# The first two chunks of a fused attention and expert kernel share each weight block, and most of the weight decoding moves behind the first batch

## The chip, the cores and the metric

The kernel runs on one core of a Trainium2 chip. Its time is the device time of one execution in microseconds; the version before took 1003.2 us (median of three runs, 1001.3 to 1006.09). A profile of one execution stands beside it. Engines are named as the profile names them: PE (matmul) with PEld (its weight loads), DVE (vector), ACT (scalar), POOL (GpSimd), and SP, which only issues transfers (SPq is its queue).

## The reference

All inputs are float32, apart from two weight matrices that arrive as float64 and are read as pairs of 32-bit words. Cut to what matters:

```python
q, k, v                                # (8 batches, 8 heads, 576, 64)
q_d, k_d, v_d = mean of 4 neighbours   # (8, 8, 144, 64)
out_up = repeat(softmax(q_d @ k_d.T / 8) @ v_d, 4)         # coarse attention
mask   = |i - j| < 4                                       # 7 neighbours
out_local = softmax(where(mask, q @ k.T / 8, -1e9)) @ v    # local attention
x = (out_up + out_local) as (4608 tokens, 512)
h = x @ w_in                           # (512, 2048)
g = max(h, 0) + alpha * min(h, 0)      # alpha: one per column
out = g @ w_out                        # (2048, 512)
```

## The kernel before, in words

**The long part** is the two products with w_in and w_out. The tokens are cut into 18 chunks of 256, the 2048 hidden columns into 8 pairs of 128-column blocks; one chunk with one pair is a *step*, 144 in all. Every number is carried as a high part and a low part, so that each product takes three matmuls. A step consists of `hidden` (L760, 24 matmuls into a tile `h`), `slopes` (L771 to L775, ACT scales `h` by the two slopes), `larger` (the greater of the two, L783, on DVE), `split` (`gh`, L788 on ACT, and `gl`, L70 on POOL) and `product` (L817, 24 matmuls into `o`, a bank for each 128 tokens). In the first 12 steps (`EARLY`) the greater of the two is not taken on DVE: ACT makes a second tile `sh` (L773) and POOL adds it (L73). After the eighth step of a chunk `finish` copies `o` to `sg` (L823, ACT) and stores it.

**The weights** have to be decoded first, w_in and w_out in eight blocks each, block (0, p) and (1, p) for pair p. `make` gives the five parts of a block: `magnitude` (L187, ACT), `reach` (L191 and L192, DVE), `bits` (L196 and L197, DVE, which read the raw words), `upper` (L202 for w_in, L206 for w_out, ACT: the high part) and `lower` (L210 or L214, DVE: the low part). A block is decoded whole (instructions of 1024 columns, with the temporary tile in SBUF) or in two halves (512 columns, temporary in a PSUM bank). Raw words come in by SP's queue (L148 for w_in, L152 for w_out, two transfers of 0.5 MB a block) into three slots; the last two pairs of blocks go to four buffers that are in the pool `late`. The memory of that pool is the first batch's until that batch is done.

**The first batch** of attention (batch 0, which is the tokens of steps 0 to 15 and a little more) runs ahead of all that, on a path of its own (`first_batch`, L399 to L525), and ends with `xh` and `xl`, the two parts of x that step 0 multiplies. Beside it DVE and ACT decode the blocks of the first `N_EARLY` pairs. Which of the early loads are queued at which place is told by the string `ORDER`: `a0` is q and k of head pair 0, `b0` its v, `i0` and `o0` the raw words of blocks (0, 0) and (1, 0).

**Later batches** are worked on between the steps: the coarse attention by `down` (folds on POOL, L73; s, pT and pv on PE), the local attention in *units* of a third of a batch (L597 to L656 on DVE). The end of a unit is its *join* (L677 on DVE, then `xh` on ACT and `xl` on POOL), which gives x for one and a half chunks. Chunk 2, which is step 16 in the order before, needs unit 3 and a part of unit 4.

**The order** behind the first batch is written out by hand: every function is put at a time counted in steps (`at(s - 1.95, hidden, s)`), all are sorted by it, and each engine runs its instructions in that order. The decoding of half blocks starts at 0.5 and a half is given 0.56; `UNITS` gives the beginnings of units 3 to 7. Nothing on an engine passes what stands ahead of it.

Of the kernel before, what the change touches and what calls it, by code (L numbers as in the profile page):

```python
# [9 lines left out]
F32 = mybir.dt.float32  # L10
# [3 lines left out]
ALU = mybir.AluOpType  # L14
# [11 lines left out]
NF = DF // 128  # L26
# [25 lines left out]
def tile_attention_moe(ctx: ExitStack, tc: tile.TileContext, q, k, v, w_in, w_out, alpha, out):  # L52
# [4 lines left out]
    two = ctx.enter_context(tc.tile_pool(name="two", bufs=2))  # L57
    PS = bass.MemoryType.PSUM
    ps_o = ctx.enter_context(tc.tile_pool(name="ps_o", bufs=2, space=PS))
    ps_h = ctx.enter_context(tc.tile_pool(name="ps_h", bufs=2, space=PS))  # L60
# [14 lines left out]
    NS = NCHUNK * NF // 2  # L75
    NP = NF // 2


# [672 lines left out]
    def hidden(st):  # L751
        c, fp = divmod(st, NP)
        xh, xl = xT[c]
        ph = hs[st] = ps_h.tile([128, 2, T], F32, tag="ph", name=f"h{st}")
        for j in range(2):
            n, o = divmod(2 * fp + j, 4)
            i = 0
            for w, x in ((wi[0][n], xh), (wi[1][n], xh), (wi[0][n], xl)):
                for m in range(4):
                    nc.tensor.matmul(ph[:, j], w[:, m, 128 * o:128 * o + 128], x[:, m, :],  # L760
                                     start=(i == 0), stop=(i == 11))
                    i += 1

    def slopes(st):
# [4 lines left out]
        for j in range(2):  # L769
            f = 2 * (st % NP) + j  # L770
            nc.scalar.activation(t[:, j], hs[st][:, j], AF.Copy, scale=slope[:, f:f + 1])  # L771
            if st < EARLY:
                nc.scalar.activation(other[:, j], hs[st][:, j], AF.Relu, scale=gain[:, f:f + 1])  # L773
            else:
                nc.scalar.activation(other[:, j], hs[st][:, j], AF.Copy, scale=sign[:, f:f + 1])  # L775
# [29 lines left out]
    def product(st):  # L805
        c, fp = divmod(st, NP)
        if fp == 0:
            outs[c] = [ps_o.tile([128, DM], F32, tag="po", name=f"o{c}_{m}") for m in range(T // 128)]
        gh, gl = gs.pop(st)
        order = [(j, i, m) for j in range(2) for i in range(3) for m in range(T // 128)]  # L810
        if st == NS - 1 or fp == 0:
            order.sort(key=lambda x: x[2])
        for j, i, m in order:
            f = 2 * fp + j
            n, o = divmod(f, 4)
            g, w = ((gh, 0), (gh, 1), (gl, 0))[i]
            nc.tensor.matmul(outs[c][m], g[:, j, 128 * m:128 * m + 128], wo[w][n][:, o, :],  # L817
                             start=(f == 0 and i == 0), stop=(f == NF - 1 and i == 2))

    def finish(c):  # L820
        for m, po in enumerate(outs.pop(c)):
            sg = two.tile([128, DM], F32, tag="stage", name=f"sg{c}_{m}", bufs=SB)
            nc.scalar.copy(sg, po)  # L823
            for i in range(4):
# [26 lines left out]
    with tc.tile_pool(name="start", bufs=1) as start:  # L851
# [26 lines left out]

    for s in range(NS):
        at(s - 1.95, hidden, s)  # L880
        at(s - 1.45, slopes, s)
        at(s - 1.15, larger, s)
        at(s - 1.0, split, s)
        at(s + 0.6, product, s)
        if s % NP == NP - 1:
            at(s + 1.02, finish if s + 1 < NS else finish_last, s // NP)

    blocks = [(w, fp, c) for w in range(2) for fp in range(N_EARLY, NP) for c in range(2)]
# [5 lines left out]
    for w, fp, c in blocks:  # L894
        for lag, f in zip((-0.3, 0.0, 0.4, 0.95, 1.2), make(w, fp, c)):
            at(t + lag * D_DEC, f)
        t += D_DEC
        if w == 0 and fp >= NP - 2:
            at(t, load_raw, 1, fp, (c,))
    decoded = t  # L900
# [6 lines left out]
    for u in range(len(UNITS) + 3, 3 * B + 1):  # L907
        begin[u] = begin[u - 1] + U_STEP
    at(3.3, load_q, 3)
    at(3.4, load_kv, 3, "k")  # L910
    at(decoded + 0.3, load_kv, 3, "v")
# [8 lines left out]
    for u in range(3, 3 * B + 1):  # L920
# [4 lines left out]
        if put and u - 1 in BY_HALF:  # L925
            flip_at(u - 1, 1, begin[u] + 0.3, flip)
            put(1, when["before 0"])
        elif put:
            flip_at(u - 1, 0, begin[u] + 0.3, flip)
            put(0, when["before 0"])  # L930
            t = when["before 0"] + 0.25 if u == 4 else when["before 1"]
            flip_at(u - 1, 1, max(begin[u] + 0.31, t - 0.6), flip)
            put(1, t)
# [56 lines left out]
```

## Time and profile before

| | |
|---|---|
| time, median of 3 runs | 1003.2 us (1001.3 to 1006.09) |
| span of the profiled execution | 995.7 us |
| PE busy in the span | 955.8 us (96%) |
| DVE | 825.6 us (83%) |
| ACT | 559.2 us (56%) |
| POOL | 497.8 us (50%) |
| last `xl` of the first batch begins on DVE | 87.11 us |
| last piece of decoding begins on DVE | 146.52 us |
| first local instruction of unit 3 begins on DVE | 147.70 us |
| first matmul of step 16 (first of chunk 2) | 191.55 us |

The time of the profiled execution is that of the first to the last instruction; the 7.5 us between it and the median lie around the span. The rows read: start, duration (both us), engine, line, operation, output and inputs, shape; in brackets the idle time ahead of it and what ended that. The windows give busy time with the number of instructions, the granted clock of PE as a share of full speed, the share of the DMA engines' time and what they moved.

### The profile page before, as it was taken

The numbers are of one execution on the slowest core, as the hardware profiler recorded it, in microseconds if no ns is written. First come the engines' busy times: TensorE is split into PE (matmuls) and PEld (weight loads), VectorE is DVE, ScalarE is ACT, GpSimd is POOL, SyncE is SP. The second block draws the span as 40 slices with busy tenths as digits, with TensorE's granted clock in tenths as the row PEclk, the third lists the DMA queues.
The fourth block names the chain that finished last, engine by engine and source line by source line (L and its number), as shares of the span: only waits on it lengthen the run. The fifth ranks groups of instructions, "written<-read, shape, count | busy, mean of one in ns | idle before, by whom it ended". The sixth has DMA issues, their size and how long they took to land.

```text
span 995.7 us, 17954 instructions
## 1 busy us (share of the span) xinstructions
PE 955.8 (96%) x6402; PEld 850.2 (85%) x6402; DVE 825.6 (83%) x1336; ACT 559.2 (56%) x1483; POOL 497.8 (50%) x624
## 2 busy tenths in 40 slices
PE   5977999999999999999999999999999999999998
PEld 4756877888889888888998889898889888899896
DVE  7999887889898889899899888899898889996111
ACT  5766775455656555555565555565556564544442
POOL 2132866677475636555546455655456632324221
PEclk9957999999999999999999999999999999999999
DMA  8947524243423322423322323232324222210000
GB/s 209 217 150 260 159 65 130 79 126 90 131 90 100 111 87 68 136 79 102 98 87 82 117 84 109 91 104 88 100 84 126 85 67 67 70 33 22 1 22 22
DMA packets 63196, 98.27 MB, mean 99 GB/s; under 512 B 23556, under 2 KB 28932, under 8 KB 63108
## 3 DMA queue, kind: packets, MB, share of 16 engines
q1 hardware_dynamic: 62916, 96.88, 33.0%
q8 instruction: 50, 0.82, 0.3%
q10 hardware_dynamic: 192, 0.26, 0.1%
q14 instruction: 38, 0.31, 0.1%
HBM read 87.67 MB, written 9.44 MB: 98 GB/s over the span
## 4 chain that ended last, share of the span: by engine, by line
PE 77%; DVE 12%; ACT 3%; POOL 3%; issue 2%; SPq 1%; DMA 1%; DVEq 0%; POOLq 0%; ACTq 0%
PE o L817 35%; PE h L760 35%; PE s L266 2%; PE pv L300 2%; PE xp L665 1%; DVE temp L196 1%; DVE lb L656 1%; PE pT L290 1%; DVE qk L597 1%; DVE temp L197 1%; DVE ls L601 1%; SPq L399 1%; POOL t L73 1%; DVE wil L210 1%; DVE pv L653 1%
## 5 line engine op out<-in xcount | busy, mean ns | idle before, releaser
L70 POOL TENSOR_TENSOR gl<-t,gh 128x512 fp32r<-128x512 f32 x144 | 186.3, 1294 | 347.2 <-ACT gh L788 340.1
L771 ACT ACTIVATE t<-h,slope 128x256 f32<-128x256 f32 x288 | 136.7, 474 | 144.7 <-PE h L760 117.5
L817 PE MATMUL o<-woh,gh 128*128 128x512 f32 x576 | 194.9, 409 | 2.6 <-ACT sg L823 2.6
L760 PE MATMUL h<-xh,wih 128*128 128x256 f32 x1152 | 189.5, 286 | 0.6 <-ACT xh L524 0.6
L817 PE MATMUL o<-wol,gh 128*128 128x512 f32 x576 | 188.2, 397 | 0.2 <-DVE wol L214 0.2
L817 PE MATMUL o<-woh,gl 128*128 128x512 f32 x576 | 187.9, 397 | 0.0
L760 PE MATMUL h<-xl,wih 128*128 128x256 f32 x1152 | 183.1, 281 | 0.8 <-POOL xl L70 0.8
L760 PE MATMUL h<-xh,wil 128*128 128x256 f32 x1152 | 183.2, 281 | 0.0
L783 DVE TENSOR_TENSOR t<-h,t 128x512 f32<-128x512 f32 x132 | 90.7, 687 | 103.0 <-ACT h L775 101.8
L760 PEld LDWEIGHTS h<-xh,wih 128*128 128x128 f32 x1152 | 163.5, 190 | 11.0 <-issue 1.0
L788 ACT CAST gh<-t 128x512 fp32r<-128x512 f32 x144 | 89.2, 619 | 127.7 <-DVE t L783 95.7
L760 PEld LDWEIGHTS h<-xl,wih 128*128 128x128 f32 x1152 | 156.3, 189 | 1.0 <-POOL xl L70 1.0
L760 PEld LDWEIGHTS h<-xh,wil 128*128 128x128 f32 x1152 | 156.4, 189 | 0.0
L73 POOL TENSOR_TENSOR ld<-ld 72x256 f32<-72x256 f32 x168 | 127.5, 759 | 42.4 <-DMA ld<-in_q 39.7
L601 DVE TENSOR_REDUCE ls<-qk 128x12 f32<-128x768 f32 (+1 forms) x126 | 136.5, 1084 | 3.2
L817 PEld LDWEIGHTS o<-woh,gl 128*128 128x128 f32 x576 | 108.7, 189 | 26.3
L817 PEld LDWEIGHTS o<-wol,gh 128*128 128x128 f32 x576 | 108.3, 188 | 26.4 <-DVE wol L214 1.4
L656 DVE TENSOR_TENSOR lb<-lb,pv 128x384 f32<-128x384 f32 x202 | 113.9, 564 | 5.6
L817 PEld LDWEIGHTS o<-woh,gh 128*128 128x128 f32 x576 | 99.6, 189 | 20.2 <-ACT sg L823 3.1
L775 ACT ACTIVATE h<-h,sign 128x256 f32<-128x256 f32 x264 | 116.1, 440 | 0.0
L653 DVE TENSOR_TENSOR pv<-v,lb 128x1152 f32<-128x1152 f32 x84 | 93.6, 1115 | 2.6
L597 DVE TENSOR_TENSOR qk<-k,qp 128x768 f32<-128x768 f32 (+1 forms) x78 | 83.9, 1076 | 0.0
(151 smaller groups left out, 1133.4 us busy)
## 6 DMA issues: line engine op xcount, KB each, us to landing
k<-in_k SPq DMA_DIRECT2D x41, 384.0 KB
v<-in_v SPq DMA_DIRECT2D x41, 384.0 KB
out<-sg SPq DMA_DIRECT2D x140, 64.0 KB
raw<-in_moe_w_in SPq DMA_DIRECT2D x16, 512.0 KB
raw<-in_moe_w_out SPq DMA_DIRECT2D x16, 512.0 KB
ld<-in_q SPq DMA_DIRECT2D x56, 144.0 KB
ld<-in_k SPq DMA_DIRECT2D x56, 144.0 KB
ld<-in_v SPq DMA_DIRECT2D x56, 144.0 KB
```

The costliest lines, as they stand in the source:

```text
L70: nc.gpsimd.tensor_tensor(o, a, b, op=ALU.subtract)
L73: nc.gpsimd.tensor_tensor(o, a, b, op=ALU.add)
L597: nc.vector.tensor_tensor(st["pr"][:, :nd], window(tiles[u, "k"], half, d0, nd), st["qp", half].unsqueeze(1).to_broadcast([128, nd, 2, 192 ...
L601: nc.vector.tensor_reduce(out=st["s"][:, half, d0:d0 + nd, :].rearrange("p a b -> p (a b)"), in_=st["pr"][:, :nd].rearrange("p a h (t d) - ...
L653: nc.vector.tensor_tensor(st["pr"][:, :nd], window4(tiles[u, "v"], half, d0, nd), prob(half, d0, nd), op=ALU.mult)
L656: nc.vector.tensor_tensor(st["acc"], st["acc"], st["pr"][:, i], op=ALU.add)
L760: nc.tensor.matmul(ph[:, j], w[:, m, 128 * o:128 * o + 128], x[:, m, :], start=(i == 0), stop=(i == 11))
L771: nc.scalar.activation(t[:, j], hs[st][:, j], AF.Copy, scale=slope[:, f:f + 1])
L775: nc.scalar.activation(other[:, j], hs[st][:, j], AF.Copy, scale=sign[:, f:f + 1])
L783: nc.vector.tensor_tensor(gs[st], hs.pop(st), gs[st], op=ALU.max)
L788: nc.scalar.copy(gh, t)
L817: nc.tensor.matmul(outs[c][m], g[:, j, 128 * m:128 * m + 128], wo[w][n][:, o, :], start=(f == 0 and i == 0), stop=(f == NF - 1 and i == 2))
```

## The change

Lines of the changed kernel are 8 higher than before (L196 becomes L204, L760 becomes L768).

- **Order of the steps.** `BLOCKS` runs chunk 0 with pairs 0 to 3, then chunk 1 with all eight pairs, then chunk 0 with pairs 4 to 7. Chunks 2 to 17 follow as before, each with a start that lies `GAP` = 2.4 later in the table.
- **Chunk 0 in two parts.** After its first four steps `park` copies the two banks of `o` (ACT) and stores them in DRAM; `fetch` loads them in the second half, and `finish` adds them on DVE where it otherwise copies on ACT.
- **Decoding.** Two blocks, (0, 0) and (0, 1), instead of ten stand ahead of the end of the first batch. Twelve blocks are decoded whole and four in halves, where it was ten and six; they come in the order in which the steps need them (`WHOLE`, `HALVES`).
- **Loads.** Only the raw words of w_in for pairs 0 to 2 are queued among the first batch's loads; each other block's are queued when the third block ahead of it has been read.
- **Attention.** Units 3 to 7 begin 3.7 to 2.4 later in the table, the join of unit 4 is put at fixed places. `EARLY` is 16 instead of 12.

```diff
-ORDER = 'i0 a0 a1 b0 o0 a2 b1 a3 b2 i1 b3 o1 i2'
-N_EARLY = 5
+ORDER = 'i0 a0 a1 b0 i1 a2 b1 a3 b2 b3 i2'
+WHOLE = ((0, 0), (0, 1), (0, 2), (1, 0), (0, 3), (1, 1), (1, 2), (1, 3), (0, 4), (0, 5), (1, 4), (1, 5))
+HALVES = ((0, 6), (0, 7), (1, 6), (1, 7))
+N_EARLY = 2
+T_DEC, D_DEC, D_HALF = -1.6, (0.6, 0.6, 0.6, 0.6, 0.86, 0.86, 0.86, 0.86, 0.86, 0.86), 0.56
+BLOCKS = [(0, 0, 4), (1, 0, 8), (0, 4, 8)]
-T0_DEC, D_DEC = 0.5, 0.56
-UNITS = {3: 7.5, 4: 12.2, 5: 17.4, 6: 22.7, 7: 28.0}
+UNITS = {3: 11.2, 4: 15.6, 5: 20.3, 6: 25.3, 7: 30.4}
+GAP = 2.4
-EARLY = 12
+EARLY = 16
...
+    blocks = BLOCKS + [(c, 0, NP) for c in range(2, NCHUNK)]
+    steps = [(c, p, p == a, p == z - 1) for c, a, z in blocks for p in range(a, z)]
...
+    def park(c):
+        parked[c] = dram.tile([128, T // 128, DM], F32, name=f"parked{c}")
+        for m, po in enumerate(outs.pop(c)):
+            sg = two.tile([128, DM], F32, tag="stage", name=f"pk{c}_{m}", bufs=SB)
+            nc.scalar.copy(sg, po)
+            nc.sync.dma_start(parked[c][:, m, :], sg)
+
+    def fetch(c):
+        for m in range(T // 128):
+            sg = back[c, m] = two.tile([128, DM], F32, tag="stage", name=f"bk{c}_{m}", bufs=SB)
+            nc.sync.dma_start(sg, parked[c][:, m, :])
+
     def finish(c):
         for m, po in enumerate(outs.pop(c)):
-            sg = two.tile([128, DM], F32, tag="stage", name=f"sg{c}_{m}", bufs=SB)
-            nc.scalar.copy(sg, po)
+            if c in parked:
+                sg = back.pop((c, m))
+                nc.vector.tensor_tensor(sg, po, sg, op=ALU.add)
+            else:
+                sg = two.tile([128, DM], F32, tag="stage", name=f"sg{c}_{m}", bufs=SB)
+                nc.scalar.copy(sg, po)
...
-        for fp in range(NP - 2):
-            for which in range(2):
-                if fp < N_EARLY:
-                    if (which, fp) not in raws:
-                        load_raw(which, fp)
-                    for f in make(which, fp):
-                        f()
+        for which, fp in WHOLE[:N_EARLY]:
+            for f in make(which, fp):
+                f()
...
-    at(-1.98, load_raw, 0, N_EARLY)
-    for fp in (NP - 2, NP - 1):
-        at(-1.97, load_raw, 0, fp)
-    at(-1.96, load_raw, 1, N_EARLY)
-    t = T0_DEC
+    at(-1.98, load_raw, 0, NP - 2)
+    at(-1.97, load_raw, 0, NP - 1)
+    t = T_DEC
+    bits_done = [-1.96] * N_EARLY
+    for (w, fp), d in zip(WHOLE[N_EARLY:], D_DEC):
+        for lag, f in zip((-0.3, 0.0, 0.4, 0.95, 1.2), make(w, fp)):
+            at(t + lag * d, f)
+        bits_done.append(t + 0.8 * d)
+        t += d
+    for i, (w, fp) in enumerate(WHOLE):
+        if (w, fp) not in raws:
+            at(bits_done[i - 3], load_raw, w, fp)
```

Three places show what moves. The first is SP's queue around the end of the first batch; `raw` is a tile of raw words, `in_moe_w_out` is w_out, `ld` a load of batch 1's attention. Before:

```order
L148 DMA raw_2_178<-in_moe_w_in 128x2x512 x2
L235 DMA ld_0_3_911<-in_k 72x512
L235 DMA ld_0_4_915<-in_v 72x512
L235 DMA ld_0_5_920<-in_v 72x512
L152 DMA raw_2_835<-in_moe_w_out 128x1024 x2
L148 DMA raw_3_849<-in_moe_w_in 128x2x512 x2
L152 DMA raw_3_859<-in_moe_w_out 128x1024 x2
L148 DMA raw_4_871<-in_moe_w_in 128x2x512 x2
L152 DMA raw_4_883<-in_moe_w_out 128x1024 x2
L148 DMA raw_5_958<-in_moe_w_in 128x2x512 x2
L148 DMA raw_60_961<-in_moe_w_in 128x2x512
```

And now:

```order
L156 DMA raw_2_174<-in_moe_w_in 128x2x512 x2
L243 DMA ld_0_0_804<-in_q 72x512
...
L156 DMA raw_60_865<-in_moe_w_in 128x2x512
L156 DMA raw_61_867<-in_moe_w_in 128x2x512
L156 DMA raw_70_869<-in_moe_w_in 128x2x512
L156 DMA raw_71_871<-in_moe_w_in 128x2x512
L160 DMA raw_0_873<-in_moe_w_out 128x1024 x2
L156 DMA raw_3_876<-in_moe_w_in 128x2x512 x2
L160 DMA raw_1_923<-in_moe_w_out 128x1024 x2
```

The four half loads of pairs 6 and 7 (`raw_60` to `raw_71`), whose buffers lie in `late`, now stand ahead of the first block of w_out (`raw_0_873`) and of all that follow; before, ten blocks stood ahead of them.

The second is DVE around the last `xl` of the first batch (L525, now L533). Before:

```order
L196 SCALAR_TENSOR_TENSOR temp<-raw_4_871,temp 128x1024
L214 SCALAR_TENSOR_TENSOR wol_844<-temp,sign,woh_843 128x512 x2
L525 TENSOR_TENSOR xl_330<-fxs_785,xh_329 128x256
L197 SCALAR_TENSOR_TENSOR temp<-raw_4_871,temp 128x1024
L191 TENSOR_SCALAR temp<-temp 128x1024
L192 TENSOR_SCALAR temp<-temp 128x1024
```

And now:

```order
L526 TENSOR_TENSOR fxs_781<-fpv_772,fod_757 128x256
L533 TENSOR_TENSOR xl_326<-fxs_781,xh_325 128x256
L199 TENSOR_SCALAR temp<-temp 128x1024
L200 TENSOR_SCALAR temp<-temp 128x1024
L218 TENSOR_TENSOR wil_927<-temp,wih_926 128x4x256
L204 SCALAR_TENSOR_TENSOR temp<-raw_0_873,temp 128x1024
L205 SCALAR_TENSOR_TENSOR temp<-raw_0_873,temp 128x1024
```

Before, the fifth pair's blocks were in work there. Now it is the first block of w_out: L199 and L200, which work on its magnitude, stand ahead of the low part of block (0, 2), `wil_927`.

The third is ACT at the same place, as it is now; `t` and `sh` are step 0's, `wih_926` and `gh_929` the high parts of block (0, 2) and of step 0's result:

```order
L532 CAST xh_325<-fxs_781 128x256
L779 ACTIVATE t_907<-h_879,slope 128x256
L781 ACTIVATE sh_908<-h_879,gain 128x256
L779 ACTIVATE t_907<-h_879,slope 128x256
L781 ACTIVATE sh_908<-h_879,gain 128x256
L195 ACTIVATE temp<-raw_0_873 128x1024
L210 CAST wih_926<-temp 128x4x256
L796 CAST gh_929<-t_907 128x512
```

The magnitude of the first block of w_out (L195) stands ahead of `wih_926` and of `gh_929`.

More of the change, by code (lines that the diff above doesn't have):

```diff
@@ L877, in tile_attention_moe @@
     late = ctx.enter_context(tc.tile_pool(name="late", bufs=1))
[L879 to L888, printed above, removed]
-    at(-1.98, load_raw, 0, N_EARLY)
-    for fp in (NP - 2, NP - 1):
-        at(-1.97, load_raw, 0, fp)
-    at(-1.96, load_raw, 1, N_EARLY)
-    t = T0_DEC
[L894 to L899, printed above, removed]
+    for s, (c, fp, opens, closes) in enumerate(steps):
+        z = s + GAP * (c >= 2)
+        at(z - 1.95, hidden, s)
+        at(z - 1.45, slopes, s)
+        at(z - 1.15, larger, s)
+        at(z - 1.0, split, s)
+        at(z + 0.6, product, s)
+        if closes:
+            if fp < NP - 1:
+                at(z + 1.02, park, c)
+            else:
+                at(z + 1.02, finish if s + 1 < NS else finish_last, c)
+        if opens and fp:
+            at(z + 2.0, fetch, c)
+    at(-1.98, load_raw, 0, NP - 2)
[10 more added lines that the diff above has]
+            at(bits_done[i - 3], load_raw, w, fp)
+    for w, fp in HALVES:
+        for c in range(2):
+            for lag, f in zip((-0.3, 0.0, 0.4, 0.95, 1.2), make(w, fp, c)):
+                at(t + lag * D_HALF, f)
+            t += D_HALF
+            if w == 0:
+                at(t, load_raw, 1, fp, (c,))
     decoded = t
@@ L927, in tile_attention_moe @@
             put(1, when["before 0"])
+        elif u == 4:
+            for i in range(2):
+                flip_at(u - 1, i, begin[u] + 0.02 + 0.01 * i, flip)
+                put(i, begin[u] + 0.45 + 0.05 * i)
         elif put:
```

26 lines of the change are left out of this document (14 added, 12 removed).

## The prediction

> **What bounds the kernel now.** I read the shares first, then the windows, then the timelines of DVE and PE around the first batch.
>
> ```profile
> PE 955.8 (96%) x6402; PEld 850.2 (85%) x6402; DVE 825.6 (83%) x1336; ACT 559.2 (56%) x1483; POOL 497.8 (50%) x624
> core 0: us, PE busy (x) PEld busy (x) DVE busy (x) ACT busy (x) POOL busy (x), PEclk, DMA share, GB/s
> 0.00:37.00 37.00, 25.69 (x172) 22.94 (x172) 29.09 (x60) 21.81 (x54) 5.63 (x26) 1.00 0.93 211
> 37.00:88.00 51.00, 38.11 (x287) 30.75 (x286) 50.67 (x87) 35.66 (x86) 13.51 (x12) 0.60 0.60 185
> 88.00:100.00 12.00, 9.54 (x69) 8.79 (x69) 10.62 (x10) 8.54 (x24) 5.91 (x4) 1.00 0.89 300
> 100.00:147.60 47.60, 44.27 (x291) 37.60 (x290) 40.88 (x64) 34.87 (x85) 34.72 (x44) 1.00 0.40 115
> 147.60:191.50 43.90, 41.59 (x268) 35.84 (x267) 34.50 (x53) 23.68 (x69) 29.52 (x37) 0.96 0.40 118
> 300.00:500.00 200.00, 200.00 (x1355) 179.63 (x1354) 178.08 (x290) 113.53 (x315) 113.08 (x148) 1.00 0.32 97
> ```
>
> PE is busy 200.00 of 200 us from 300 on, so a shift of the steps there goes to the end whole. What can change lies ahead of chunk 2, where DVE is the engine that is full: 50.67 of 51 us up to 88, PE's clock there 0.60. These are the marks:
>
> ```profile
> 81.65 0.58 PE L760 MATMUL h<-xh,wih 128*128 128x256 f32 x1 [0.65 <-ACT xh L524]
> 86.73 1.01 PE L760 MATMUL h<-xh,wih 128*128 128x256 f32 x4
> 87.11 0.42 DVE L525 TENSOR_TENSOR xl<-fxs,xh 128x256 fp32r<-128x256 f32 x1
> 146.52 0.75 DVE L214 SCALAR_TENSOR_TENSOR wol<-temp,sign,woh 128x512 fp32r<-128x512 f32 x1 [0.76 <-ACT woh L206]
> 147.70 1.34 DVE L597 TENSOR_TENSOR qk<-k,qp 128x1152 f32<-128x1152 f32 x1
> 187.03 1.25 DVE L677 TENSOR_TENSOR xf<-xp,od 128x256 f32<-128x256 f32 x3
> 191.56 0.74 POOL L70 TENSOR_TENSOR xl<-xf,xh 128x256 fp32r<-128x256 f32 x1 [1.26 <-ACT xh L691]
> 191.55 0.73 PE L760 MATMUL h<-xh,wih 128*128 128x256 f32 x4
> ```
>
> Step 0 begins at 81.65, step 1 at 86.7, the first batch's last `xl` at 87.11, decoding ends at 147.3, unit 3 begins behind it at 147.7, its join is at 187.0 and step 16 (chunk 2) begins at 191.55, at the join's end. So this is one chain on DVE: first batch, decoding, unit 3, join, step 16. I forecast when step 16 begins; everything behind it has the same steps in both.
>
> **First batch.** Ahead of the last `xl` DVE now decodes three blocks up to their `bits` instead of ten. A whole block's five instructions read:
>
> ```profile
> 63.33 1.21 DVE L197 SCALAR_TENSOR_TENSOR temp<-raw,temp 128x1024 int32<-128x1024 int32 x1
> 64.46 0.68 DVE L191 TENSOR_SCALAR temp<-temp 128x1024 f32<-128x1024 f32 x1
> 65.80 0.68 DVE L192 TENSOR_SCALAR temp<-temp 128x1024 int32<-128x1024 int32 x1
> 66.52 1.15 DVE L210 TENSOR_TENSOR wil<-temp,wih 128x1024 fp32r<-128x1024 f32 x1
> 68.46 1.21 DVE L196 SCALAR_TENSOR_TENSOR temp<-raw,temp 128x1024 int32<-128x1024 int32 x1
> 85.78 1.41 DVE L214 SCALAR_TENSOR_TENSOR wol<-temp,sign,woh 128x512 fp32r<-128x512 f32 x2
> ```
>
> Added up that is 4.9 us for a block of w_in (L191, L192, L196, L197, L210) and 5.2 for one of w_out (L214 for L210), a little less where an instruction begins before the last one has ended (1.21 after 63.33 is 64.54, the next starts at 64.46). I take 4.8 and 5.0; six to seven blocks less are some 30 us. Not all of it comes off: the end of the batch is also a chain through PE and ACT.
>
> ```profile
> 53.70:81.60 27.90, 17.51 (x133) 12.06 (x131) 27.57 (x45) 19.32 (x44) 5.35 (x7) 0.50 0.59 199
> ```
>
> In this stretch PE has 17.5 us of work at half clock. With DVE out of the way the batch can't end before 53.7 + 17.5 = 71.2. I take 71.2, which is **16 us earlier**. Bounds: 57.5 if all of DVE's 30 us came off, 87 if none did. The Trainium skill, page "TensorE: Matmul & The Clock Gate", Part 1, says that PE runs at half clock until it has been busy for about 3.4 us without a break; the 0.50 agrees. By that rule a batch that fed PE without gaps would run at the full clock; 53.7 + 8.8 = 62.5 would come out.
>
> **The first block of w_out.** Before, its words were loaded among the first batch's. Now it stands on SP behind the half loads of pairs 6 and 7, whose buffers are free only when the last `xl` has run. That wait is in the trace of before, where it held up nothing but those loads:
>
> ```profile
> SPq L148 <- DVE xl L525: 2.8, 1, 2.8
> 80.16 1.16 ACT L187 ACTIVATE temp<-raw 128x1024 f32<-128x1024 f32 x1 [1.51 <-DVE wil L210]
> ```
>
> So 4 transfers of 0.5 MB and then the 2 of that block, 3.1 MB, start at the last `xl`. At the 300 GB/s of the window from 88 that is **10.5 us** (9.3 if the DMA share were 1.0 instead of the 0.89 there; 15 at the 211 of the first window). Then comes its magnitude, 1.16 on ACT: **1.2 us**. What stands behind that magnitude on ACT is the high part of block (0, 2) and `gh` of step 0, and on DVE its L199 and L200 stand ahead of the low part of (0, 2). So step 2, which needs that block, and the first `product` wait too, and DVE idles some 11 us. Two `hidden` are all that PE has in this time, and one took 5.1 us at 81.65.
>
> **Decoding from there.** Three blocks of w_in and six of w_out whole: 3 x 4.8 + 6 x 5.0 = 44.4. The low part of (0, 2): 1.1. Eight halves:
>
> ```profile
> 114.66 0.69 DVE L191 TENSOR_SCALAR temp<-temp 128x512 f32<-128x512 f32 x1
> 117.91 0.69 DVE L191 TENSOR_SCALAR temp<-temp 128x512 f32<-128x512 f32 x1
> 147.18 0.59 DVE L270 TENSOR_REDUCE dnb<-s 96x3 f32<-96x432 f32 x1
> ```
>
> They follow one another every 3.25, so 26. Four pairs of the coarse attention of batch 1 add 0.59 each (L270), 2.4. Sum **74 us**. It is work which the first batch had beside it before, and now PE's steps wait on it in the order of need.
>
> **What this DVE work loses.** Before, in the 59.6 us from 88 to 147.6, DVE was idle 8.1 us (12.00 - 10.62 and 47.60 - 40.88) over some 12 half blocks and a piece of a whole one, waiting for ACT. Besides, whole blocks keep their temporary in SBUF. When POOL worked beside them:
>
> ```profile
> 88.58 0.69 DVE L191 TENSOR_SCALAR temp<-temp 128x1024 f32<-128x1024 f32 x1
> 89.55 1.56 POOL L73 TENSOR_TENSOR t<-sh,t 128x512 f32<-128x512 f32 x1 [29.55 <-ACT sh L773]
> 91.84 1.48 POOL L70 TENSOR_TENSOR gl<-t,gh 128x512 fp32r<-128x512 f32 x1 [0.73 <-ACT gh L788]
> 94.09 1.47 POOL L73 TENSOR_TENSOR t<-sh,t 128x512 f32<-128x512 f32 x1 [0.77 <-ACT sh L773]
> 90.03 2.17 DVE L196 SCALAR_TENSOR_TENSOR temp<-raw,temp 128x1024 int32<-128x1024 int32 x1
> 92.12 2.29 DVE L210 TENSOR_TENSOR wil<-temp,wih 128x1024 fp32r<-128x1024 f32 x1
> 94.33 2.31 DVE L197 SCALAR_TENSOR_TENSOR temp<-raw,temp 128x1024 int32<-128x1024 int32 x1
> ```
>
> The same three instructions that took 1.21, 1.15 and 1.21 alone took 2.17, 2.29 and 2.31, each with one of POOL's in it; so each can lose 1.0 to 1.1. L191 and L192, with one input, lost nothing (0.69 at 88.58 as at 64.46), and the halves, whose temporary is in PSUM, run at 0.69. Before, nearly all whole blocks were done when POOL was still idle (29.55 us ahead of its first `t`); now nine of twelve come while POOL makes `t` and `gl` of the steps. With three such instructions a block, 27 of them are exposed, so up to 27 to 28 us, with 8 to 10 of waits for ACT beside it: bounds 0 and 37. POOL is busy 34.72 of 47.6 us there, in part on folds that wait for nothing, but a collision also puts it off. I take a third of the 27 and half of the waits, **13 us**.
>
> By the Trainium skill, page "SBUF — State Buffer", section "SBUF: two separate sides", an instruction of DVE with two inputs in SBUF and one of GpSimd share a pair of ports, which the first to start holds whole while the other fully blocks. The rows agree. By this rule alone every one of the 27 that meets POOL would lose up to one of POOL's instructions; the sum would be 14 us more if all did.
>
> Decoding then ends at 71.2 + 10.5 + 1.2 + 74 + 13 = **169.9**, where it was 147.3.
>
> **From unit 3 to step 16.** Before: 191.55 - 147.3 = 44.3. Of it go: the idle 5.07 in
>
> ```profile
> 166.95 0.32 DVE L622 TENSOR_REDUCE lb<-lex 128x12 f32<-128x84 f32 x1 [5.07 <-ACT lex L617]
> 171.83 0.69 DVE L783 TENSOR_TENSOR t<-h,t 128x512 f32<-128x512 f32 x1 [1.24 <-ACT h L775]
> 184.71 0.94 DVE L597 TENSOR_TENSOR qk<-k,qp 128x768 f32<-128x768 f32 x1
> 186.17 0.94 DVE L601 TENSOR_REDUCE ls<-qk 128x12 f32<-128x768 f32 x1
> ```
>
> since ACT's queue has little ahead of L617 once the steps' work is behind it; three `larger` of 0.69 (L783), which are POOL's now that `EARLY` is 16; and 1.9 of unit 4 (L597, L601) that stand ahead of the join. The two adds of the returned chunk come in, about 1.3 by the row of L783, which has the same shape. 44.3 - 5.1 - 2.1 - 1.9 + 1.3 = **36.5** (34 to 44). The 1.9 and one `larger` less come back behind the join as 1.2.
>
> Step 16 thus begins at 169.9 + 36.5 = 206.4, against 191.55: +14.9, and with the 1.2 the end comes **16 us** later. PE can't win that back, since its work of 16 steps, which it did by 191.5 before, is done by then and it idles until the join.
>
> **What costs nothing.** Parking moves 2 x 0.25 MB out and in again, under 4 us of the DMA engines, whose share is 0.40 there; its two copies on ACT run while DVE decodes:
>
> ```profile
> L823 ACT COPY sg<-o 128x512 f32<-128x512 f32 x34 | 18.1, 585 | 0.0
> ```
>
> What covers them is ACT's free time, 47.60 - 34.87 = 12.7 us from 100 to 147.6; if that were gone, twice 0.585, 1.2 us, would be added to what DVE waits for. The sums on DVE are in the 36.5. The order of the steps in itself adds no matmul.
>
> So the span is 995.7 + 16 = 1011.7, and with the 7.5 around it, which I leave as it is, the time is 1003.2 + 16 = **1019 us**.
>
> **The rivals.**
>
> 1. *PE becomes the bound of the first sixteen steps (other side).* Decoding keeps up with the steps because they share blocks, which is one block for two steps. Then only PE counts: what it did from 81.65 to 191.5 (9.54 + 44.27 + 41.59 from the windows and some 6 before 88, about 101 us busy) begins at 71, waits some 6 us for the first block of w_out once two `hidden` are done, and is done at 178 to 179. Step 16 at 179 is 12 us earlier: **991**. For it: DVE's 74 us from 83 fit into 157 without any loss, and unit 3 in 34. Its point: decoding must end before about 149 with the batch's end near 62, or unit 3 must get into the gaps. Against: the three doubled rows, and DVE idle for ten of these microseconds.
> 2. *It cancels.* Batch at 64, loads 10, losses 8: decoding ends at 64 + 10 + 1.2 + 74 + 8 = 157.2, step 16 at 193.7, which is +2 and with the 1.2 **1006**.
> 3. *The batch isn't shorter, so that the change doesn't do what it says.* PE, ACT or loads of k and v hold it: last `xl` at 82 instead of 71, all else as in the sum: +11, **1030**. For it: DMA share 0.93 up to 37, clock 0.50 in the stretch. Against: DVE's 27.57 of 27.9 busy there.
> 4. *Nearly every two-input instruction of the nine blocks meets POOL.* 25 us for 13 in the losses: +12, **1031**.
>
> **How the numbers follow.** Forecast 0.52 (1010 to 1030 by itself), rival 1 0.15, rival 2 0.16, rival 3 0.08, rival 4 0.09. Half a per cent, 5 us, is about what a measurement of this kernel can tell from no change: 998 to 1008. Faster: 0.15, from rival 1. Same: 0.16, rival 2, and 0.01 of the forecast's lower edge. Slower: the rest, 0.68. The terms' own bounds come to -14 and +16 (batch), -1 and +5 (loads), -13 and +24 (losses), -3 and +8 (unit 3); as independent errors 19 down and 30 up at the utmost. The range goes from 997, which leaves out the better part of rival 1, to 1034, past rivals 3 and 4: about 0.1 is left out below and 0.07 above.
>
> **What will show it.** The last `xl` (now L533) at 69 to 75 is the first term; later, rival 3. SP's wait for it, with some 10 us to the landing of `raw` by L160 behind it, and DVE idle ahead of a L199 for about 11 us is the second. Means of L204, L205 and L218 of 1024 columns near 1.5 to 1.6 (1.15 to 1.21 alone) are the losses; at 2 rival 4, at 1.2 to 1.3 rival 1. The first L605 of unit 3 (L597 before) at 165 to 175, and step 16 at 200 to 212. From 300 on each step must take as long as before; if it doesn't, the reasoning that all lies ahead of step 16 is wrong. I am also wrong if the steps' `hidden` and DVE's work pass each other otherwise than the chain says, so that step 16 doesn't begin at the join's end.

## The result, and the profile after

The changed kernel takes 1050.3 us (median of five runs, 1044.8 to 1051.9) where the kernel before, in runs beside it, takes 1001.3 us: a ratio of 1.0477 (95% interval 1.0435 to 1.0518), 47 to 49 us slower (47.3 by the spans, 49.0 by the medians). The direction was forecast, the size was not: 16 us were expected, and 1034 was the upper end of the range. The profiled execution has a span of 1043.0 us, 47.3 more than before.

The marks of the prediction, from the timelines of DVE and PE of the changed kernel (not all of its lines are 8 higher: POOL's L75 and L78 are L70 and L73 of before, L824 is L817):

```profile
69.73 0.42 DVE L533 TENSOR_TENSOR xl<-fxs,xh 128x256 fp32r<-128x256 f32 x1 [0.47 <-ACT xh L532]
83.28 0.69 DVE L199 TENSOR_SCALAR temp<-temp 128x1024 f32<-128x1024 f32 x1 [13.13 <-ACT temp L195]
190.63 0.75 DVE L222 SCALAR_TENSOR_TENSOR wol<-temp,sign,woh 128x512 fp32r<-128x512 f32 x1 [0.25 <-ACT woh L214]
193.76 1.36 DVE L605 TENSOR_TENSOR qk<-k,qp 128x1152 f32<-128x1152 f32 x1 [1.65 <-ACT qp L599]
226.00 1.17 DVE L685 TENSOR_TENSOR xf<-xp,od 128x256 f32<-128x256 f32 x3
230.35 1.01 PE L768 MATMUL h<-xh,wih 128*128 128x256 f32 x3 [2.32 <-ACT xh L699]
```

The chain is the one that was forecast: last `xl` at 69.7, a hole of 13.1 us on DVE, decoding until 191.4, unit 3, join, step 16 at 230.35. Step 16 is 38.8 us later than before (191.55), and 8.5 more are lost behind it. The windows between these marks:

```profile
53.70:70.10 16.40, 14.43 (x150) 11.61 (x150) 10.34 (x29) 10.57 (x34) 0.91 (x3) 0.80 0.00 1
70.10:83.30 13.20, 4.16 (x37) 3.94 (x35) 0.07 (x2) 2.74 (x6) 1.28 (x1) 0.78 0.93 341
83.30:157.20 73.90, 55.62 (x299) 46.44 (x300) 66.20 (x54) 42.40 (x91) 50.14 (x38) 0.85 0.39 133
157.20:191.40 34.20, 27.47 (x172) 23.93 (x171) 28.97 (x46) 24.33 (x63) 18.94 (x21) 0.95 0.42 137
230.30:395.40 165.10, 155.32 (x1015) 138.43 (x1016) 141.16 (x231) 87.60 (x253) 101.86 (x134) 0.96 0.33 99
```

They show four things. The first batch's end is no longer DVE's: it is busy 10.34 of 16.4 us, PE 14.43 at a clock of 0.80. Nothing is loaded then (DMA share 0.00), and behind it everything at once (0.93) while DVE stands still. The nine whole blocks fill 83.3 to 157.2, with DVE busy 66.2 us where the sum allowed some 46. And the last row, which holds 24 steps, is 165.1 us long; before, the same 24 steps took 348.2 - 191.6 = 156.6. Behind step 40 both kernels need the same 647.6 us.

The hole is the wait that was forecast. SP waits for the last `xl`, ACT for the words of the first block of w_out:

```profile
SPq L156 <- DVE xl L533: 19.1, 1, 19.1
82.13 1.12 ACT L195 ACTIVATE temp<-raw 128x1024 f32<-128x1024 f32 x1 [9.44 <-DMA raw<-in_moe_w_out]
```

The stretched instructions show when DVE's groups are taken for the window of the nine whole blocks (line, shape, count, busy, mean ns), with one of POOL's behind them:

```profile
L204 DVE SCALAR_TENSOR_TENSOR temp<-raw,temp 128x1024 int32<-128x1024 int32 x9 | 16.2, 1805 | 0.0
L205 DVE SCALAR_TENSOR_TENSOR temp<-raw,temp 128x1024 int32<-128x1024 int32 x9 | 16.0, 1780 | 0.3
L222 DVE SCALAR_TENSOR_TENSOR wol<-temp,sign,woh 128x512 fp32r<-128x512 f32 x10 | 11.7, 1205 | 0.6 <-ACT woh L214 0.6
L199 DVE TENSOR_SCALAR temp<-temp 128x1024 f32<-128x1024 f32 x9 | 9.2, 1026 | 18.0 <-ACT temp L195 18.0
L200 DVE TENSOR_SCALAR temp<-temp 128x1024 int32<-128x1024 int32 x9 | 8.5, 939 | 0.3
L218 DVE TENSOR_TENSOR wil<-temp,wih 128x1024 fp32r<-128x1024 f32 x4 | 5.1, 1284 | 1.6 <-ACT wih L210 1.6
L78 POOL TENSOR_TENSOR ld<-ld 72x256 f32<-72x256 f32 x12 | 15.4, 1286 | 0.4 <-DMA ld<-in_q 0.4
```

Alone L204, L205 and L218 take 1.21 us, L222 0.70 (half of the 1.41 for two), L199 and L200 0.68. What the busy times hold above that is the stretch: in the order of the rows, 5.3 + 5.1 + 4.7 + 3.1 + 2.3 + 0.3 = 20.8 us. Each stretched instruction has an instruction of POOL in it, as here:

```profile
138.61 1.77 DVE L199 TENSOR_SCALAR temp<-temp 128x1024 f32<-128x1024 f32 x1
138.33 1.49 POOL L75 TENSOR_TENSOR gl<-t,gh 128x512 fp32r<-128x512 f32 x1 [0.73 <-ACT gh L796]
139.79 1.17 POOL L78 TENSOR_TENSOR ld<-ld 72x256 f32<-72x256 f32 x1
```

L199 is an instruction with one input, and it took 1.77 instead of 0.68. Which of the two loses goes by which began first:

```profile
88.08 1.23 DVE L205 SCALAR_TENSOR_TENSOR temp<-raw,temp 128x1024 int32<-128x1024 int32 x1
88.54 1.91 POOL L78 TENSOR_TENSOR t<-sh,t 128x512 f32<-128x512 f32 x1 [1.57 <-ACT sh L781]
89.23 1.77 DVE L199 TENSOR_SCALAR temp<-temp 128x1024 f32<-128x1024 f32 x1
```

L205 began ahead of POOL's instruction and kept its time, L199 began while that one ran. Over the six groups of DVE in this window, 30 of the 31 instructions that began while one of POOL's ran are stretched, and none of the 8 that began first and were met by POOL later. It is the same the other way round: the 11 first additions of a fold that began while one of these DVE instructions ran took 1.17 to 1.72 us, the one that began first 0.74.

### The profile page after: what moved, and what is told of

Same layout as the page of the kernel before. It is cut to its first block, busy times and chain, and to the rows that moved or that the text cites. A ratio compares the mean times of both kernels' runs of the same rounds, so it can differ in the third digit from the quotient of the medians.

```text
span 1043.0 us, 17925 instructions
## 1 busy us (share of the span) xinstructions
PE 965.9 (93%) x6402; PEld 858.6 (82%) x6402; DVE 842.1 (81%) x1325; ACT 558.5 (54%) x1480; POOL 519.6 (50%) x628
## 4 chain that ended last, share of the span: by engine, by line
PE 76%; DVE 8%; POOL 4%; ACT 4%; DMA 3%; issue 2%; SPq 2%; ACTq 0%; POOLq 0%; DVEq 0%
PE h L768 34%; PE o L824 34%; PE s L274 2%; PE pv L308 1%; DMA raw<-in_moe_w_in 1%; PE xp L673 1%; PE pT L298 1%; DVE lb L664 1%; POOL ld L78 1%; DMA raw<-in_moe_w_out 1%; DVE pv L661 1%; POOL t L78 1%; SPq L407 1%; POOL gl L75 1%; DVE temp L204 1%
## 5 line engine op out<-in xcount | busy, mean ns | idle before, releaser
L75 POOL TENSOR_TENSOR gl<-t,gh 128x512 fp32r<-128x512 f32 x144 | 188.5, 1309 | 375.7 <-ACT gh L796 362.4
L824 PE MATMUL o<-woh,gh 128*128 128x512 f32 x576 | 197.7, 414 | 4.6 <-ACT woh L214 2.5
L768 PE MATMUL h<-xh,wih 128*128 128x256 f32 x1152 | 191.4, 288 | 6.3 <-ACT wih L210 3.8
L824 PE MATMUL o<-wol,gh 128*128 128x512 f32 x576 | 190.0, 400 | 2.3 <-DVE wol L222 2.3
L824 PE MATMUL o<-woh,gl 128*128 128x512 f32 x576 | 189.4, 399 | 1.3 <-POOL gl L75 1.3
L768 PE MATMUL h<-xl,wih 128*128 128x256 f32 x1152 | 184.1, 282 | 3.9 <-POOL xl L75 3.9
L768 PE MATMUL h<-xh,wil 128*128 128x256 f32 x1152 | 185.6, 283 | 0.5 <-DVE wil L218 0.5
L768 PEld LDWEIGHTS h<-xh,wih 128*128 128x128 f32 x1152 | 165.6, 192 | 17.1 <-ACT wih L210 4.3
L791 DVE TENSOR_TENSOR t<-h,t 128x512 f32<-128x512 f32 x128 | 88.0, 687 | 102.0 <-ACT h L783 101.2
L768 PEld LDWEIGHTS h<-xl,wih 128*128 128x128 f32 x1152 | 157.3, 190 | 4.1 <-POOL xl L75 4.1
L768 PEld LDWEIGHTS h<-xh,wil 128*128 128x128 f32 x1152 | 158.8, 192 | 0.7 <-DVE wil L218 0.7
L78 POOL TENSOR_TENSOR ld<-ld 72x256 f32<-72x256 f32 x168 | 132.2, 787 | 37.1 <-DMA ld<-in_q 37.1
L824 PEld LDWEIGHTS o<-wol,gh 128*128 128x128 f32 x576 | 109.8, 191 | 29.7 <-DVE wol L222 4.3
L824 PEld LDWEIGHTS o<-woh,gl 128*128 128x128 f32 x576 | 109.3, 190 | 28.2 <-POOL gl L75 1.7
L824 PEld LDWEIGHTS o<-woh,gh 128*128 128x128 f32 x576 | 100.8, 191 | 23.2 <-issue 3.0
L783 ACT ACTIVATE h<-h,sign 128x256 f32<-128x256 f32 x256 | 112.6, 440 | 0.0
```

What stands on the lines that cost most here:

```text
L75: nc.gpsimd.tensor_tensor(o, a, b, op=ALU.subtract)
L78: nc.gpsimd.tensor_tensor(o, a, b, op=ALU.add)
L791: nc.vector.tensor_tensor(gs[st], hs.pop(st), gs[st], op=ALU.max)
```

## The experiments

Each ratio is against the kernel before, run beside it on the same chip. In profiles the last `xl` of the first batch comes up to 6 us earlier or later from run to run with little or nothing changed ahead of it, so traces are compared by distances from that mark. In the runs that add the sharing to the kernel before, lines up to the steps are 4 higher than there (L191 and L195 are its L187 and L191).

| run | time | ratio to before, 95% interval | end of last `xl` to end of decoding | step 16 to step 40 |
|---|---|---|---|---|
| kernel before | | | 59.7 | 156.6 |
| changed kernel | 1050.3 | 1.0477 (1.0435 to 1.0518) | 121.2 | 165.0 |
| changed kernel again | 1048.8 | 1.0465 (1.0428 to 1.0502) | 120.9 | 164.5 |
| half loads later | 1035.1 | 1.0349 (1.0321 to 1.0378) | 113.3 | 164.5 |
| nine blocks in halves | 1036.3 | 1.0370 (1.0342 to 1.0397) | 110.7 | 164.5 |
| both | 1030.7 | 1.0309 (1.0281 to 1.0338) | 104.3 | 166.4 |
| POOL's pieces small | 1037.6 | 1.0350 (1.0319 to 1.0381) | 110.2 | 166.0 |
| half loads later, units earlier | 1029.1 | 1.0270 (1.0229 to 1.0310) | 113.2 | 156.9 |
| all mended | 1018.1 | 1.0179 (1.0148 to 1.0210) | 102.1 | 156.9 |
| decoding beside the first batch | 1005.8 | 1.0044 (1.0025 to 1.0064) | 64.6 | 157.3 |
| before, sharing alone | 1002.3 | 1.0033 (1.0017 to 1.0049) | 64.7 | 157.7 |
| before, sharing, own tile for parking | 999.2 | 0.9978 (0.9961 to 0.9995) | 61.1 | 157.6 |
| before, EARLY = 16 | 1002.5 | 1.0021 (1.0004 to 1.0038) | 59.5 | 155.8 |
| before, sharing, own tile, EARLY = 16 | 999.6 | 0.9986 (0.9968 to 1.0004) | 59.6 | 156.6 |

**The changed kernel again,** as a control:

> The changed kernel once more, on the chip of the next three. All theories: 1045 to 1050 (its profiled span was 1043.0).

1048.8 us, ratio 1.0465, span 1045.1. Its last `xl` ended at 73.1 instead of 70.2, and all distances behind that mark agree within 0.5 us.

**The half loads later.**

```diff
-    at(-1.98, load_raw, 0, NP - 2)
-    at(-1.97, load_raw, 0, NP - 1)
+    at(0.0, load_raw, 0, NP - 2)
+    at(0.01, load_raw, 0, NP - 1)
```

> The changed kernel with the four half loads of pairs 6 and 7 issued later (at 0.0 of the table instead of -1.98), so that the first block of w_out and those behind it are loaded without waiting for the last xl of the first batch. Theory A (the words of w_out come late, and collisions with POOL stretch the decoding): DVE's idle time of 13.1 us ahead of the first L199 behind the last xl falls under 3, step 16 begins at about 219 instead of 230, and the time is some 11 us less, 1039. Rival B (the steps' order, the parking and PE's waits set the time, decoding only follows): the idle time moves elsewhere and the time stays within 3 us of 1050.

The time fell to a ratio of 1.0349, 1.2% below the changed kernel. The hole on DVE fell from 13.13 to 5.09 us, not under 3, and step 16 came at 222.0:

```profile
74.89 0.86 DVE L199 TENSOR_SCALAR temp<-temp 128x1024 f32<-128x1024 f32 x1 [5.09 <-ACT temp L195]
72.25 0.47 ACT L779 ACTIVATE t<-h,slope 128x256 f32<-128x256 f32 x1 [2.91 <-PE h L768]
73.69 1.16 ACT L195 ACTIVATE temp<-raw 128x1024 f32<-128x1024 f32 x1
```

The words are there now, but the magnitude stands behind the four instructions of step 0's slopes on ACT, which wait for `h`: this order was covered by the late words and shows when they are gone. Rival B falls.

**The nine blocks in halves,** with the temporary in PSUM.

```diff
-        for lag, f in zip((-0.3, 0.0, 0.4, 0.95, 1.2), make(w, fp)):
-            at(t + lag * d, f)
+        for c in range(2):      # from the second block of this list on
+            for lag, f in zip((-0.3, 0.0, 0.4, 0.95, 1.2), make(w, fp, c)):
+                at(t + lag * d / 2, f)
+            t += d / 2
```

> The changed kernel with the nine blocks behind (0, 2) decoded in halves, with their temporary in PSUM instead of SBUF. Theory A: the instructions go back to 0.69 each whether POOL runs beside them or not, a half takes 3.25 plus waits; 18 halves are 59 us where the nine whole blocks took 74, step 16 begins 8 to 14 us earlier and the time is about 1040. Rival C (ACT's queue, in which magnitude and high part wait their turn, sets the pace of decoding; the stretching only fills time that would be idle): DVE's idle time between 83 and the end of decoding rises by what the stretching loses, and the time stays at 1047 to 1055.

Decoding ended 10.5 us earlier (110.7 from the mark instead of 121.2); 2.0 of that is a shorter hole (11.15 for 13.13). The ratio is 1.0370. The groups of the halves, and the window they come from, in which POOL is busy 47 of 88 us:

```profile
86.60:175.00 88.40, 69.30 (x392) 59.48 (x393) 78.92 (x123) 60.90 (x147) 47.09 (x56) 0.87 0.49 165
L204 DVE SCALAR_TENSOR_TENSOR temp<-raw,temp 128x512 int32<-128x512 int32 x23 | 15.7, 685 | 0.0
L200 DVE TENSOR_SCALAR temp<-temp 128x512 int32<-128x512 int32 x24 | 16.8, 700 | 0.8
```

685 and 700 ns are what they take alone, and the other groups show the same: nothing is stretched. DVE's idle time behind the hole went down, from 12.9 to 10.6 us, where rival C had it rise. Though halves need more instructions, DVE's busy time from the last `xl` to the end of decoding fell from 95.2 to 88.9 us.

**Both edits:**

> Both edits, the later half loads and the halves in PSUM. Theory A: the two add up, some 20 us less than the changed kernel, about 1029; what then remains over the kernel before is DVE work that stood beside the first batch and now stands in the path. Rival B: no change against 1050. Rival C: as with the loads alone, about 1039.

104.3 us from the mark: 16.9 less than the changed kernel, where the two alone gave 7.9 and 10.5. By this distance they nearly add up. By the time they do so only in part: the ratio, 1.0309, is 0.017 below the changed kernel's, where the two alone took off 0.013 and 0.011.

**POOL's pieces small.** This puts POOL's part to the test without touching DVE's instructions.

```diff
-            add(lv[:, :, 0:128], lv[:, :, 0:128], lv[:, :, 128:256])
+            n = 8 if b == 1 else 128
+            add(lv[:, :, 0:n], lv[:, :, 0:n], lv[:, :, 128:128 + n])
...
-            add(gs[st], hs.pop(st), gs[st])
+            other = hs.pop(st)
+            add(gs[st][:, :, 0:8], other[:, :, 0:8], gs[st][:, :, 0:8])
```

> The changed kernel with two kinds of POOL's instructions cut to 8 columns: the addition of sh to t in the first 16 steps, and the first addition of each fold of batch 1. This leaves that part of the computation out (the activation of chunks 0 and 1 and the coarse attention of batch 1). DVE, ACT and PE have the same instructions as before. Some 27 of POOL's 50 us between 83 and 157 go. Theory A (DVE's decoding is stretched by POOL's instructions, 20.8 us in the nine whole blocks): more than half of the stretch goes, the means of L204 and L205 fall from 1.8 to 1.4 us or less, decoding ends 11 to 16 us earlier, and so do step 16 and the end: some 1033. Rival C (ACT's queue sets the pace): the instructions are shorter but the waits longer; decoding ends within 3 us of where it did.

```profile
L204 DVE SCALAR_TENSOR_TENSOR temp<-raw,temp 128x1024 int32<-128x1024 int32 x9 | 14.3, 1590 | 0.0
L205 DVE SCALAR_TENSOR_TENSOR temp<-raw,temp 128x1024 int32<-128x1024 int32 x9 | 12.7, 1409 | 0.3
L222 DVE SCALAR_TENSOR_TENSOR wol<-temp,sign,woh 128x512 fp32r<-128x512 f32 x10 | 7.4, 784 | 0.6 <-ACT woh L214 0.6
L199 DVE TENSOR_SCALAR temp<-temp 128x1024 f32<-128x1024 f32 x9 | 7.0, 773 | 18.0 <-ACT temp L195 18.0
L78 POOL TENSOR_TENSOR ld<-ld 72x16 f32<-72x16 f32 x12 | 9.5, 792 | 0.0
```

DVE's busy time fell by 13.0 us (95.2 to 82.2), its idle time rose by 2.0, decoding ended 10.7 to 11 us earlier, just at or below the lower edge of what was expected; the ratio is 1.0350. The same DVE instructions, beside smaller instructions of POOL, are shorter: POOL is the cause of the stretch. L204 still has a mean of 1590 ns, above the 1400 expected, since `gl` and the second additions of the folds were left as they are: the stretched ones of L204 and L205 all began while one of these ran.

**Units 4 to 6 earlier,** with the half loads later.

```diff
-UNITS = {3: 11.2, 4: 15.6, 5: 20.3, 6: 25.3, 7: 30.4}
+UNITS = {3: 11.2, 4: 15.1, 5: 19.8, 6: 25.1, 7: 30.4}
```

> The changed kernel with the later half loads (as in the experiment on the loads) and units 4 to 6 earlier in the table: 15.1, 19.8 and 25.1 for 15.6, 20.3 and 25.3. That is the distance to the steps which they had before. Theory D (the 8 us that the changed kernel loses between step 16 and step 40 come from the places of units 4 to 6 in the table): step 40 comes 157 to 159 us behind step 16 instead of 164.5, the time is 5 to 8 us less than with the later loads alone. Rival E (they come from unit 4 starting 40 us later than before on a DVE that is full, while PE has already done its two products): step 40 comes 163 to 166 us behind step 16 and the time stays.

Theory D holds: 156.9 us from step 16 to step 40 instead of 164.5, and 1.0270 where the later loads alone gave 1.0349. The largest single wait of PE that goes is in the first step of chunk 3, which multiplies what the join of a unit gives. First the changed kernel, then this one (PE, and POOL, which makes `xl`):

```profile
291.46 0.74 PE L768 MATMUL h<-xl,wih 128*128 128x256 f32 x4 [3.87 <-POOL xl L75]
289.46 1.27 POOL L75 TENSOR_TENSOR gl<-t,gh 128x512 fp32r<-128x512 f32 x1
290.68 1.15 POOL L75 TENSOR_TENSOR xl<-xf,xh 128x256 fp32r<-128x256 f32 x2
295.88 0.60 DVE L278 TENSOR_REDUCE dnb<-s 96x3 f32<-96x432 f32 x1 [5.80 <-PE s L274]
```

```profile
279.29 0.74 PE L768 MATMUL h<-xl,wih 128*128 128x256 f32 x4 [0.86 <-POOL xl L75]
278.50 1.15 POOL L75 TENSOR_TENSOR xl<-xf,xh 128x256 fp32r<-128x256 f32 x2
280.83 1.29 POOL L75 TENSOR_TENSOR gl<-t,gh 128x512 fp32r<-128x512 f32 x1
```

In the changed kernel `gl` of a step stands ahead of `xl` on POOL, PE waits 3.87 us, and DVE, whose next instruction wants PE's `s`, 5.80. With the units half a step earlier `xl` comes first and the wait is down to 0.86, as in the kernel before (0.82). The other 4 to 5 us of the 7.6 were not traced one by one.

**Decoding beside the first batch:** the change without its first part.

```diff
-ORDER = 'i0 a0 a1 b0 i1 a2 b1 a3 b2 b3 i2'
+ORDER = 'i0 a0 a1 b0 i1 a2 b1 a3 b2 i2 b3 o0'
-N_EARLY = 2
+N_EARLY = 10
...
-UNITS = {3: 11.2, 4: 15.6, 5: 20.3, 6: 25.3, 7: 30.4}
-GAP = 2.4
+UNITS = {3: 7.5, 4: 12.2, 5: 17.4, 6: 22.7, 7: 28.0}
+GAP = 0.0
```

> The change without its first part: ten blocks are decoded ahead of the end of the first batch again, in the order of need, with two whole blocks and eight halves behind it; units, their distance from the steps and the join of unit 4 as before. Shared blocks, parking, EARLY = 16 and 12 whole blocks stay. Theory A (what costs is that nine whole blocks were moved from beside the first batch, where POOL idles and DVE fills its gaps, into the steps): nearly all of the 47 us come back, 996 to 1008; a few us better than before are possible, since EARLY = 16 and four halves less take some 5 us off DVE. Rival B: 1020 or more.

1.0044: all but some 4 of the 47 us come back, some 8 of them by the places of the units, which this edit sets back too (157.3 us from step 16 to step 40). A gain over the kernel before, which I had thought possible, did not come.

**Sharing alone,** on the kernel before:

```diff
+BLOCKS = [(0, 0, 4), (1, 0, 8), (0, 4, 8)]
...
+            if fp < NP - 1:
+                at(s + 1.02, park, c)
...
+        if opens and fp:
+            at(s + 2.0, fetch, c)
```

> The kernel before with the new order of the steps alone: chunk 0 in two parts with parking, the decoding, its order, the loads, the units and EARLY as before. Theory A: the order of the steps by itself costs nothing that can be measured; 998 to 1007, within 0.5% of the kernel before. Rival B (sharing with parking is itself what costs): 1015 or more.

1.0033, within the half per cent but with an interval above 1. Decoding took 64.7 us from the mark instead of 59.7. Two rows say why:

```profile
131.39 0.59 ACT L829 COPY pk<-o 128x512 f32<-128x512 f32 x1 [6.20 <-DMA parked<-pk]
132.53 0.70 DVE L195 TENSOR_SCALAR temp<-temp 128x512 f32<-128x512 f32 x1 [5.43 <-ACT temp L191]
```

There are two staging tiles, and one holds the rest of batch 0 until `place_rest`, so the second bank's copy waits on ACT until the first one's store has landed, with the magnitudes behind it.

**A tile of its own for the second bank:**

```diff
-            sg = two.tile([128, DM], F32, tag="stage", name=f"pk{c}_{m}", bufs=SB)
+            sg = late.tile([128, 6, 2, 64], F32, tag="x", ...) if m else two.tile(...)
```

> The kernel before with the new order of the steps, as in the experiment on sharing alone, but the second parked bank is copied into a tile that is free until unit 3, instead of the single staging tile that is left while the other holds the rest of batch 0. Theory F (the 4 us that sharing alone cost by step 16 are ACT waiting 6.20 us for the first parked tile's store, with DVE idle 5.43 us behind it): the wait goes, step 16 comes 3 to 5 us earlier than with sharing alone (190.5 to 192.5 with the same start), the time is within 0.2% of the kernel before. Rival G (the order of the weights and steps costs it): the time stays 0.3% above the kernel before.

The wait is gone from ACT, DVE's idle time behind the mark fell from 12.9 to 9.5 us, and the ratio is 0.9978 (0.9961 to 0.9995): about 0.2% faster than the kernel before, and the fastest version here, though it can't be told from the one with EARLY = 16 added to it (0.9986). From the last `xl` to step 16 it needs 102.1 us, sharing alone 105.7, the kernel before 104.0. Step 16 itself was at 195.6 in its profile, since that execution's `xl` was late (93.5); the theory stands on the distances and the medians.

**EARLY = 16 on the kernel before:**

```diff
-EARLY = 12
+EARLY = 16
```

> The kernel before with EARLY = 16: in steps 12 to 15 POOL adds and DVE takes no larger. This is a part of the change by itself. Theory A (step 16 is set by the sum of DVE's work ahead of it): three to four instructions of 0.69 less, step 16 and the end 2 to 3 us earlier, 0.2 to 0.3% faster. Rival: ACT or POOL, which get this work, are waited for instead, and the time is the same within 0.1% or longer.

My theory fell: 1.0021, 0.2% slower. The end of decoding to step 16 took 48.8 us instead of 44.3. The join now waits on DVE:

```profile
194.38 1.27 DVE L677 TENSOR_TENSOR xf<-xp,od 128x256 f32<-128x256 f32 x3 [3.40 <-POOL t L73]
```

`sh` of the early steps lies in the tile `xf` that the join writes, so the join waits until POOL has added it. From the end of decoding to step 16 DVE is busy 0.5 us less than before (34.4 for 34.9) and idle 5.0 more: this wait, and 2.3 us in which the first instruction of unit 4 waits for ACT's `qp`.

**Sharing with a tile of its own, and EARLY = 16:**

> Sharing with a tile of its own for the parking, and EARLY = 16. If both theories hold: 2 to 3 us less than the kernel before, 0.2 to 0.3% faster. If one of the two falls: the same as before within 0.15%.

0.9986 (0.9968 to 1.0004): one of the two had fallen, and the time is that of the kernel before. The join's wait for POOL, 3.4 us, is in its trace too.

**All mended:**

> The changed kernel with all that the runs found: half loads later, nine blocks in halves, units 4 to 6 earlier, and a tile of its own for the second parked bank. Theory A: the gains add up in part (15 and 4.4 and 6 us from the runs so far, and about 1 for the parking): about 1023, still some 20 us over the kernel before, which is DVE's work that no longer lies beside the first batch. Rival: 1005 or less, which would say that nothing but these repairable faults costs.

1.0179: better than the 1023 expected, and far from 1005. Decoding ends 102.1 us behind the last `xl` with DVE busy 88.8 of them; before, it was 59.7 with 51.7 busy. Step 16 comes 138.4 us behind the last `xl` instead of 104.0, and the last `xl` is 13.8 us earlier than before: 34.4 - 13.8 = 20.6 us, which is all but 0.1 of the difference of the spans (1016.2 and 995.7).

## Why the prediction was wrong

The span grew by 47.3 where 16 was forecast; the terms account for the 31.

- **First batch:** 71.2 forecast, 70.2 measured. Its reason was half right. DVE was no longer the bound, but PE ran at 0.80 of its clock, not at 0.50, and was busy 14.43 of 16.4 us instead of 17.5 without a gap; that the sum of the two came out so near is in part luck. PE was busy 88% of this stretch, where it was 63% of the one before, and the clock went up with it. The Trainium skill, "TensorE: Matmul & The Clock Gate", Part 1, lets sustained work bring the full clock; these two stretches agree.
- **Words of w_out:** 11.7 with the magnitude, 13.1 measured. The wait and its place were right. The words landed 12.0 us after the last `xl`. Up to then some 4.0 MB had moved, more than the 3.1 up to the end of that block in the queue: loads issued behind it seem to have moved beside it.
- **DVE's work:** 74 us forecast; 95.2 measured less the stretch of 20.8 is 74.4.
- **Losses: this is the step that failed.** 13 us were taken, 33.7 measured: 20.8 of stretch and 12.9 of waits, where 9 and 4 to 5 were taken. The bounds (0 and 37) held it, the choice of a third did not. Of the waits, 8.3 us are L199 for its magnitude; no run took them away by themselves. The stretch by POOL is shown: it shrinks with POOL's instructions and is absent when the temporary is in PSUM. Two errors made it too small. The sum let only three instructions of a block be hit, on the row of L191 at 88.58; that instruction had ended at 89.27, before POOL's first began at 89.55, so the row could not show it. The next one, L192 at 89.30 (its row of before stands below), was met by POOL's and kept its time, but it had begun first. L199 and L200 lost 5.4 us; the kinds that were counted lost 15.4, where a third of 27 was taken. And POOL's own instructions stretch too (the first addition of a fold has a mean of 1286 ns here, and 733 in 88 to 148 before), so that POOL was busy 50 of 74 us and offered more to collide with. The Trainium skill, "SBUF — State Buffer", section "SBUF: two separate sides", names beside instructions with two inputs in SBUF also those of DVE in a two-port mode, which I had left out; by "VectorE: DVE Perf Modes", section "Mode 2×_2P — use both read ports for one tensor", a one-input instruction on float32 in SBUF is one. The traces agree: L199 works off 1024 columns in 0.68 us alone, the two-input ones need 1.21, and L199 is stretched by POOL as they are.

```profile
89.30 0.69 DVE L192 TENSOR_SCALAR temp<-temp 128x1024 int32<-128x1024 int32 x1
```

- **Unit 3 to step 16:** 36.5 forecast, 39.0 measured; within its bounds. The wait of 5.07 that the sum took off whole was still 2.02, and 1.65 of waiting for `qp` came in ahead of unit 3.
- **Behind step 16:** 1.2 forecast, 8.5 measured. I had taken "the same steps in both" for the same time. The table's places of units 4 to 6 had moved against the steps, and the run with the units earlier gave 7.6 us back.
- **"What costs nothing":** the parking did cost. In the changed kernel ACT waits 2.17 us for the first store, in sharing alone 6.20:

```profile
140.91 0.59 ACT L833 COPY pk<-o 128x512 f32<-128x512 f32 x1 [2.17 <-DMA parked<-pk]
```

The free time of ACT that I named as cover does not help where one tile has to be free; the tile was not looked up.

Measured less forecast, from the first batch to the time behind step 16: -1.0 + 1.4 + 0.4 + 20.7 + 2.5 + 7.3 = 31.3.

Of the rivals, "PE becomes the bound", "it cancels" and "the batch isn't shorter" did not happen. "Nearly every two-input instruction meets POOL" was the nearest: the kinds that it names lost 15.4 us by it, not 25, but all losses, for which its 25 stood, came to 33.7, and nothing stood for the time behind step 16. The range took the terms' errors as independent, which gave 30 up by its own working, 1049, and was still ended at 1034; and it had no bounds for the time behind step 16 at all.

What the change set out to do it did: shared blocks are needed half as often, and the first batch is 17 us shorter. The cost is that DVE's work between the last `xl` and the end of decoding grew from 51.7 us (some 3 of them stretch) to 74.4 without its stretch (88.8 in halves, which are not stretched). Beside the first batch it had held that batch up by 17 us at most; here every step waits for it.

## What to carry to other kernels

Work that runs beside another chain is worth moving only for what that chain gives back: here the blocks taken out from beside the first batch shortened it by 14 to 17 us, and lengthened the way from its end to step 16 by 56 us (160.2 against 104.0), or by 34.4 with all mended. When vector work moves to where another engine is busy, take the price of an instruction from a row that overlaps that engine, and check that the row really does and which of the two began first. A table of hand-set places has to be moved as a whole: half a step between units and steps was 7.6 us, and one staging tile that was still taken turned a free copy into 4 us.

## What was not expected of the hardware

An instruction of DVE with one input in SBUF is stretched by POOL as well (1.77 us instead of 0.68), and POOL by DVE: a fold's addition cut from 128 to 8 columns a row still took 792 ns on average, though the shortest took 0.21 us, and a full one that runs undisturbed 733 ns on average. In the traces the one that begins second loses. The same DVE work in halves, with its temporary in PSUM, kept its time alone (means of 682 to 700 ns, and 744 for L222) while POOL was busy 47 of 88 us. Loads issued behind one another in one queue seem to have moved side by side: a block landed when some 4.0 MB had moved (12.0 us of a stretch at 341 GB/s), though only 3.1 MB stood up to its end in the queue. No run put that to the test by itself.
